# Block sums of the spatial weights: one more set moved up behind the second weight of the first projection

## The chip, the cores and the metric

The kernel runs on one core of one Trainium2 chip. The metric is the device time of one execution in microseconds (us). Engines are named as in the profile: PE is the matrix engine, DVE the vector engine, ACT the scalar engine, POOL the GpSimd engine, SP the engine that here only issues transfers.

## The reference, cut to what matters

```
xn  = layernorm(x)                                   # 2048 x 512
s   = local dilated attention(xn, wqkv) @ wo         # 32 heads, 8 taps at distance 2
z   = gelu(xn @ w_in)                                # 2048 x 1792, halves of 896
z1, z2 = z[:, :896], layernorm(z[:, 896:])
g   = w_sp @ z2 + b_sp                               # w_sp is 2048 x 2048
out = x + s * silu((z1 * g) @ w_out)
```

Everything is float32. The kernel gets that precision by cutting each operand in a high and a low part and by three matmuls for each product.

## The kernel before, in words

The work on PE comes in this order: the projections to q, k and v; the **first projection** (z1, the loop over `f` in seven weights `w1_0` to `w1_6`, lines 693 to 713); the second projection (z2, `z2_half`); the product with `w_sp`, whose 2 x 2 blocks are multiplied in seven products instead of eight (`block_product`), for which sums of weight blocks are needed; the product with `w_out`; the product with `wo`. Attention itself is elementwise work on DVE and POOL, given the lowest priority, and fills DVE wherever nothing else is due there.

**Sets of block sums.** A set `(a, i)` of `block_sums` loads four 128 x 512 blocks of `w_sp` with two transfers of 512 KB each (tiles `sa` and `sb`, line 398, issued by SP), makes four sums on DVE (line 393) and stores the two tiles in `sums_d` (line 403, issued by POOL). `z1_sums` lists eight such sets, `(0, 0)` to `(0, 7)`; set 0 stands ahead of the loop over `f`, the others behind the turns of that loop. They are read back much later, in the products `m6`, `m7`, `m5` and `m3`. Other sets (`a` = 1) are made earlier by POOL (`pool_sums`) and, two of them, during z2 (`raw_sums`).

**The z1 tiles.** A turn `f` makes four products of 12 matmuls each, one for each `c`, every one in a bank of its own of the eight PSUM banks (`mm` goes round them). ACT takes each out with a Gelu (line 707) into half of a tile `z1t_f_0` (c = 0, 1) or `z1t_f_2` (c = 2, 3), and each full tile is stored in `z1_d` (line 709; the profile calls it `z_d`). I number the products n = 4 f + c. Product n + 8 uses the bank of product n, and the first z2 product is n = 28.

**The slots.** The tiles `sa`, `sb`, `z1t` and later `zt` (z2 before its norm) share one pool of eight slots of 512 KB, `t4`. A slot comes free when the last reader is through, which for all but `zt` is the store to memory. The program's order of instructions is set when it is built: each engine's list is filled in the order of the source (attention last), by a planner that works with modelled times, and a free slot goes to the first in that order that can use one. On the chip each engine then works through its list in order, and a tile waits for the slot that the planner gave it. In the kernel before, the program's buffer addresses give this succession ("z20" is `z1t_2_0`, "s2a" the tile `sa` of set 2; behind the arrow the tile that had the slot before):

```
first tenants: s0a s0b z00 z02 s1a s1b z10 z12
s2a<-z00  s2b<-z02  z20<-z10  z22<-s0a  s7a<-s1a  s7b<-z12  s3a<-s0b  s3b<-s1b
z30<-z20  z32<-z22  s4a<-s2a  s4b<-z30  z40<-s2b  z42<-z32  s5a<-s7a  s5b<-s7b
z50<-s3a  z52<-s3b  s6a<-z40  s6b<-z42  z60<-z50  z62<-z52  zt0<-s4a  zt8<-s4b
```

Of the kernel before, what the change touches and what calls it, by code (L numbers as in the profile page):

```python
# [24 lines left out]
FB = FH // P  # L25
# [32 lines left out]
def kernel(  # L58
# [96 lines left out]
    def mm(name):  # L155
        return ps.tile([P, 512], F32, tag=f"bank{next(turn)}", name=name)
# [15 lines left out]
    def side_pair(name):  # L172
        return [wts.tile([P, CT], F32R, tag=f"w{n}", name=name + n) for n in "hl"]

    def prep(src, n, name, raw=None, pair_=None):
        if raw is None:
            raw = fetch(src, n, name)
        hi, lo = pair_ or weight_pair(name)
        split(hi[:, :n], lo[:, :n], raw[:, :n])
        return hi, lo  # L180
# [214 lines left out]
    def block_sums(a, i, tile_=None, eng=nc.vector, loads=nc.sync, stores=nc.scalar, behind=None):  # L395
        top, low = [(tile_ or t4)(f"s{n}_{a}_{i}") for n in "ab"]
        for t, r in ((top, 0), (low, HT)):
            ins = loads.dma_start(t, w_sp[2 * a : 2 * a + 2, r + i].rearrange("c p t -> p c t"))
            if behind:
                tc.add_manual_dep(ins.ins, behind[0].ins.name, behind[1], reason="sums later")  # L400
        added([top[:, 0], top[:, 1], low[:, 0], low[:, 1]], eng)
        for r, t in enumerate((top, low)):
            stores.dma_start(sums_d[a, r, i], t)
# [15 lines left out]
    z1_sums = [(0, i) for i in range(HT)]  # L419
# [104 lines left out]
    def t4(name, n=2):  # L524
        t = wide.tile([P, 2 * CT], F32, tag="t4", name=name, bufs=WIDE)
        return t.rearrange("p (i t) -> p i t", i=2)[:, :n]
# [161 lines left out]
    def first_sums(a, i):  # L688
        block_sums(a, i, stores=nc.gpsimd)
# [3 lines left out]
    for f in range(FB):  # L693
        pair_ = side_pair("w1_last") if f == FB - 1 else None
        wh, wl = prep(w_in1[:, f, :], KB * P, f"w1_{f}", pair_=pair_)
        for c in range(NC):
            pz = mm(f"z1_{f}_{c}")
            for k in range(KB):
                cc = slice(k * P, (k + 1) * P)
                xh, xl = [planes[:, FB - KB + k, c * JC : (c + 1) * JC, a] for a in range(2)]  # L700
                nc.tensor.matmul(pz, wh[:, cc], xh, start=k == 0, stop=False)
                nc.tensor.matmul(pz, wh[:, cc], xl, start=False, stop=False)
                nc.tensor.matmul(pz, wl[:, cc], xh, start=False, stop=k == KB - 1)
            if c % 2 == 0:
                zp = t4(f"z1t_{f}_{c}")
            zt = zp[:, c % 2]
            nc.scalar.activation(zt, pz, AF.Gelu_apprx_tanh)  # L707
            if c % 2:
                nc.scalar.dma_start(z1_d[f, c - 1 : c + 1].rearrange("c p t -> p c t"), zp)
        if f == 2:  # L710
            first_sums(*z1_sums[FB])
        if f < FB - 1:
            first_sums(*z1_sums[f + 1])

    HALF = (slice(0, 512), slice(512, FH))
    WID = (512, FH - 512)
# [119 lines left out]
    for n in range(8):  # L836
        a, f = n // 2 % 2, n // 4 * 2 + n % 2
# [339 lines left out]
```

## Time and profile before

| what | value |
|---|---|
| median of 3 runs | 698.64 us (696.42 to 698.93) |
| the profiled execution: its own time | 696.63 us |
| the profiled execution: span | 694.8 us, so 1.83 us lie around the span |
| mean granted PE clock | 0.999 |
| busy share of the span | PE 99%, DVE 90%, ACT 40%, POOL 31% |
| moved by DMA | 182.36 MB, 262 GB/s on the mean over the span |

A row of the timeline gives the start, the duration, the engine, the line, the operation, output and input, the count, and in square brackets how long the engine had been idle before it and what it had waited for. `SPq` and `ACTq` rows are transfers being issued. A row of the windows gives, for a stretch of the span, its length, then the busy time of each engine with the count of instructions, the granted PE clock, the busy share of the DMA engines and the rate. A row of the waits gives the total in us, how often, and the longest.

### The profile page before, as it was taken

How to read it: one execution, taken by the hardware profiler on the slowest of the kernel's cores; microseconds unless marked ns; L12 is line 12 of the kernel's file. 1: busy time of each engine (PE TensorE's matmuls, PEld its weight loads, DVE VectorE, ACT ScalarE, POOL GpSimd, SP SyncE). 2: the span in 40 equal slices, each digit the busy share in tenths (PEclk: the TensorE clock that was granted, in tenths of full speed). 3: DMA queues.
4: the chain of work that ended last, by engine and by line, in shares of the span. 5: the costliest groups of instructions: out<-in, count | busy, mean ns of one | idle time of the engine just before them, and what ended most of it. 6: DMA issues, size and time to landing. Idle time of an engine off the chain costs nothing.

```text
span 694.8 us, 9233 instructions
## 1 busy us (share of the span) xinstructions
PE 688.0 (99%) x3084; PEld 572.9 (82%) x3084; DVE 624.9 (90%) x866; ACT 276.2 (40%) x458; POOL 213.3 (31%) x242
## 2 busy tenths in 40 slices
PE   8999999999999999999999999999999999999998
PEld 7888888888888899977888888888888887888886
DVE  6777877999999989899999998999998999999875
ACT  4343333314424256765533544342433444211432
POOL 3105737282343321223123222214021111452320
PEclk9999999999999999999999999999999999999999
DMA  8869899959999865266798878667576683645797
GB/s 269 253 191 303 273 361 374 334 200 352 406 410 363 320 227 189 96 212 221 260 401 281 289 222 305 203 224 264 158 255 215 221 306 118 242 155 167 253 339 267
DMA packets 102223, 182.36 MB, mean 262 GB/s; under 512 B 9184, under 2 KB 45280, under 8 KB 102176
## 3 DMA queue, kind: packets, MB, share of 16 engines
q1 hardware_dynamic: 56624, 102.21, 43.7%
q0 software_dynamic: 13824, 52.24, 20.8%
q10 hardware_dynamic: 31728, 27.33, 11.6%
q8 instruction: 24, 0.39, 0.2%
q14 instruction: 23, 0.19, 0.1%
HBM read 122.42 MB, written 59.32 MB: 262 GB/s over the span
## 4 chain that ended last, share of the span: by engine, by line
PE 68%; DVE 15%; DMA 8%; issue 4%; ACT 3%; POOL 1%; DVEq 0%; ACTq 0%; POOLq 0%; SPq 0%
PE g L823 35%; PE qkv L385 4%; PE qkv L387 4%; PE qkv L386 4%; PE b L1066 4%; PE b L1065 4%; PE b L1067 4%; DMA sb<-in_w_sp 3%; DVE lg L580 2%; DVE pr L573 2%; PE s L1066 2%; PE s L1067 2%; PE s L1065 2%; DMA sums_d<-sb 2%; PE qkv L308 2%
## 5 line engine op out<-in xcount | busy, mean ns | idle before, releaser
L631 POOL TENSOR_TENSOR pv<-pv 128x1024 f32<-128x1024 f32 x29 | 69.6, 2400 | 97.1 <-DVE pv L620 85.1
L573 DVE TENSOR_TENSOR pr<-k,q 128x2048 f32<-128x2048 f32 x32 | 73.6, 2300 | 4.3 <-DMA k<-qkv_d 4.1
L620 DVE TENSOR_TENSOR pv<-v,lg 128x2048 f32<-128x2048 f32 x32 | 74.6, 2331 | 0.9 <-DMA v<-qkv_d 0.4
L580 DVE TENSOR_REDUCE lg<-pr 128x128 f32<-128x2048 f32 x32 | 73.0, 2280 | 0.1
L645 POOL DMA_DIRECT2D o_d<-tt x32 | 18.0, 562 | 141.4 <-DVE tt L644 140.9
L433 ACT ACTIVATE stage<-qkv 128x512 f32<-128x512 f32 x40 | 23.0, 590 | 29.7 <-DMA qkv_d<-stage 19.7
L805 POOL DMA_DIRECT2D ol<-o_d x32 | 17.7, 555 | 36.8 <-DVE BIG L197 11.0
L707 ACT ACTIVATE z1t<-z 128x512 f32<-128x512 f32 x28 | 15.5, 596 | 28.9 <-DMA z_d<-z1t 13.5
L728 PE MATMUL z<-w_0h,BIG 128*128 128x512 f32 x64 | 25.0, 391 | 0.8 <-ACT zt L731 0.8
L1076 ACT ACTIVATE bt<-b 128x512 f32<-128x512 f32 x16 | 9.3, 594 | 39.8 <-PE b L1067 39.8
L730 PE MATMUL z<-w_0h,BIG 128*128 128x512 f32 x64 | 25.0, 391 | 0.0
L729 PE MATMUL z<-w_0l,BIG 128*128 128x512 f32 x64 | 25.0, 391 | 0.0
L752 ACT ACTIVATE zt<-zt,nmz,mvz 128x896 f32<-128x896 f32 x16 | 17.5, 1131 | 18.5 <-POOL nmz L746 18.5
L740 DVE BATCH_NORM_STATS2 zst<-zt 128x6 f32<-128x448 f32 x32 | 19.3, 613 | 6.1 <-ACT zt L731 6.0
L280 DVE TENSOR_TENSOR xT<-xT,mr 128x512 f32<-128x512 f32 x20 | 13.8, 688 | 11.8 <-DMA mr<-mv_d 6.8
L636 DVE TENSOR_TENSOR pv<-pv 128x512 f32<-128x512 f32 x32 | 22.9, 716 | 0.0
L731 ACT ACTIVATE zt<-z 128x512 f32<-128x512 f32 (+1 forms) x32 | 15.9, 536 | 14.2 <-DMA sums_d<-sa 12.8
L730 PE MATMUL z<-w_1h,BIG 128*128 128x384 f32 x64 | 21.5, 336 | 0.0
L728 PE MATMUL z<-w_1h,BIG 128*128 128x384 f32 x64 | 21.5, 335 | 0.0
L729 PE MATMUL z<-w_1l,BIG 128*128 128x384 f32 x64 | 21.4, 335 | 0.0
L195 ACT ACTIVATE BIG<-zl 128x512 fp32r<-128x512 f32 x20 | 12.4, 629 | 22.4 <-DVE zl L893 20.6
L393 POOL TENSOR_TENSOR sb<-sa,sb 128x512 f32<-128x512 f32 x12 | 18.7, 1560 | 5.3 <-DMA sb<-in_w_sp 5.0
(478 smaller groups left out, 2303.6 us busy)
## 6 DMA issues: line engine op xcount, KB each, us to landing
qkv_d<-stage ACTq DMA_DIRECT2D x24, 512.0 KB
v<-qkv_d POOLq DMA_DIRECT2D x14, 704.0 KB, 5.3
k<-qkv_d POOLq DMA_DIRECT2D x13, 704.0 KB, 6.4
sums_d<-sa POOLq DMA_DIRECT2D x14, 512.0 KB, 7.5
sums_d<-sb POOLq DMA_DIRECT2D x14, 512.0 KB, 7.8
z_d<-z1t ACTq DMA_DIRECT2D x14, 512.0 KB
zl<-z_d SPq DMA_DIRECT2D x12, 512.0 KB
tr<-t_d SPq DMA_DIRECT2D x12, 384.0 KB
```

What stands on the lines that cost most here:

```text
L385: nc.tensor.matmul(pq, xh[:, k], wh, start=k == 0, stop=False)
L573: line(nc.vector.tensor_tensor(pr, taps(ks[u], j0), qb.unsqueeze(1).to_broadcast([P, W, NJ * CS]), op=ALU.mult))
L580: line(nc.vector.tensor_reduce(lgs[u][:, :, j0 * HS : (j0 + NJ) * HS], pr.rearrange("p w (i d) -> p w i d", d=DH), axis=AX.X, op=ALU.add,))
L620: line(nc.vector.tensor_tensor(pv.rearrange("p w (i d) -> p w i d", d=DH), taps(vs[u], j0).rearrange("p w (i d) -> p w i d", d=DH), lgs[u] ...
L631: eng.tensor_tensor(pv[:, 0:4], pv[:, 0:4], pv[:, 4:8], op=ALU.add)
L728: nc.tensor.matmul(pz, xh[:, k], wh, start=k == 0, stop=False)
L729: nc.tensor.matmul(pz, xh[:, k], wl, start=False, stop=False)
L730: nc.tensor.matmul(pz, xl[:, k], wh, start=False, stop=k == KB - 1)
L823: nc.tensor.matmul(pg, z[a], w[b], start=start and i == 0, stop=stop and i == 2, skip_group_check=seeded)
L1065: nc.tensor.matmul(pp[:, cols], hi, wh, start=k == 0, stop=False)
L1066: nc.tensor.matmul(pp[:, cols], hi, wl, start=False, stop=False)
L1067: nc.tensor.matmul(pp[:, cols], lo, wh, start=False, stop=k == n - 1)
```

## The change: which set stands behind which weight

The order of the eight sets in the source becomes 0 1 2 6 3 7 4 5; before it was 0 1 2 7 3 4 5 6. Behind the turns of the loop stand:

| behind the weight `f` | 0 | 1 | 2 | 3 | 4 | 5 | 6 |
|---|---|---|---|---|---|---|---|
| before | 1 | 2 | 7, 3 | 4 | 5 | 6 | none |
| after | 1 | 2, 6 | 3, 7 | 4 | 5 | none | none |

```diff
-        if f == 2:
-            first_sums(*z1_sums[FB])
-        if f < FB - 1:
+        if f < FB - 2:
             first_sums(*z1_sums[f + 1])
+        if f in (1, 2):
+            first_sums(*z1_sums[f + FB - 2])
```

The work itself is the same: eight sets, the same transfers, the same sums, the same matmuls.

## The prediction, as put on record

> **What bounds the kernel now.** I read the page's head, then busy time by stretches and the waits of PE, then ACT, SP and POOL in order of time through the first projection.
>
> ```profile
> span 694.8 us, 9233 instructions
> PE 688.0 (99%) x3084; PEld 572.9 (82%) x3084; DVE 624.9 (90%) x866; ACT 276.2 (40%) x458; POOL 213.3 (31%) x242
> ...
> 0.00:21.75 21.75, 20.00 (x93) 16.45 (x94) 14.84 (x40) 9.21 (x14) 6.57 (x14) 1.00 0.88 290
> 21.75:230.00 208.25, 208.25 (x928) 172.82 (x927) 178.64 (x213) 69.93 (x121) 90.63 (x90) 1.00 0.91 318
> 230.00:240.00 10.00, 9.22 (x47) 8.05 (x46) 9.86 (x13) 2.19 (x5) 3.49 (x3) 1.00 1.00 399
> 240.00:290.00 50.00, 50.00 (x249) 44.84 (x248) 44.31 (x94) 31.30 (x50) 11.16 (x21) 1.00 0.51 178
> 290.00:330.00 40.00, 39.10 (x176) 32.08 (x175) 37.36 (x60) 26.96 (x45) 11.39 (x12) 1.00 0.58 188
> 330.00:690.00 360.00, 360.00 (x1591) 297.44 (x1589) 338.22 (x446) 136.64 (x226) 90.05 (x102) 1.00 0.73 247
> 690.00:694.80 4.80, 1.38 (x13) 1.23 (x11) 1.70 (x4) 0.00 (x0) 0.00 (x0) 0.82 0.31 109
> ...
> PE z L728 <- ACT zt L731: 0.8, 1, 0.8
> ```
>
> The first number behind the length is PE's busy time. PE has no gap from 21.75 to 230, from 240 to 290 and from 330 to 690. Its idle time is 1.75 us at the head, 0.78 from 230 to 240, 0.90 from 290 to 330 and 3.42 at the tail. Head and tail are out of this change's reach, so the most that it could give back is 0.78 + 0.90 = 1.68 us, or 0.24%, and only the 0.78 lies in the stage that it touches. What it can cost has no such bound: PE runs on only while ACT empties the banks in time, and ACT waits for slots of `t4`.
>
> ```profile
> 175.91 1.09 ACT L707 ACTIVATE z1t<-z 128x512 f32<-128x512 f32 x2 [9.64 <-DMA z_d<-z1t]
> 182.63 0.60 ACT L707 ACTIVATE z1t<-z 128x512 f32<-128x512 f32 x1 [5.63 <-DMA sums_d<-sa]
> ...
> 187.83 1.09 ACT L707 ACTIVATE z1t<-z 128x512 f32<-128x512 f32 x2
> ...
> 204.21 1.09 ACT L707 ACTIVATE z1t<-z 128x512 f32<-128x512 f32 x2 [8.36 <-DMA sums_d<-sb]
> ...
> 216.31 1.09 ACT L707 ACTIVATE z1t<-z 128x512 f32<-128x512 f32 x2
> ...
> 236.70 0.98 ACT L731 ACTIVATE zt<-z 128x512 f32<-128x512 f32 x2 [12.08 <-DMA sums_d<-sa]
> ```
>
> These are n = 8 and 9 (z20), 10 (z22), 12 and 13 (z30), 16 and 17 (z40), 20 and 21 (z50), then zt0. Three of the waits end with a store of block sums; the last of them is what stalls PE for 0.78 us, just before ACT starts on zt0 at 236.70. When a bank is due is read from the first matmul of a weight, the number ahead of "to":
>
> ```profile
> L701 PE MATMUL z<-BIG,w_2h x16: 389/389/389, 162.7 to 172.9; 128*128 128x512 f32 x16
> L701 PE MATMUL z<-BIG,w_4h x16: 389/389/389, 184.5 to 194.7; 128*128 128x512 f32 x16
> L701 PE MATMUL z<-BIG,w_5h x16: 389/389/389, 195.4 to 205.6; 128*128 128x512 f32 x16
> L701 PE MATMUL z<-BIG,w_lasth x16: 389/389/389, 206.2 to 216.4; 128*128 128x512 f32 x16
> ...
> L728 PE MATMUL z<-w_0h,BIG x64: 387/389/502, 217.1 to 290.6; 128*128 128x512 f32 x64
> ```
>
> From weight 2 (n = 8, 162.7) to the first z2 product (n = 28, 217.1) are 20 products in 54.4 us, 2.72 us each. Bank n is due when product n + 8 starts, and it is empty one ACT step (0.60) after the wait ends. So the reserve is 184.5 - 176.5 = 8.0 us at n = 8, 195.4 - 188.4 = 7.0 at n = 12, 206.2 - 204.8 = 1.4 at n = 16 and 217.1 - 216.9 = 0.2 at n = 20. PE doesn't stall there, but at n = 16 and 20 it nearly does. The z1 stage is not short of matmul time; it is short of slots.
>
> **The change part by part.** Work: nothing is added or removed. A set is two issues on SP, four sums on DVE and two issues on POOL:
>
> ```profile
> 185.24 0.37 SPq L398 DMA_DIRECT2D sa<-in_w_sp  x1
> 185.71 0.44 SPq L398 DMA_DIRECT2D sb<-in_w_sp  x1
> ...
> 198.74 0.42 SPq L398 DMA_DIRECT2D sa<-in_w_sp  x1
> ...
> 221.77 0.38 SPq L398 DMA_DIRECT2D sa<-in_w_sp  x1
> ...
> 193.56 0.99 DVE L393 TENSOR_TENSOR sb<-sa,sb 128x512 f32<-128x512 f32 x1
> ...
> 175.56 1.14 POOL L403 DMA_DIRECT2D sums_d<-sa  x2 [0.79 <-DVE sa L393]
> ...
> 189.71 0.54 POOL L403 DMA_DIRECT2D sums_d<-sa  x1
> ...
> 194.96 0.53 POOL L403 DMA_DIRECT2D sums_d<-sb  x1 [0.44 <-DVE sb L393]
> ...
> DMA to landing us min/median/max: 2.9/9.1/11.7
> ...
> 170.00:230.00 60.00, 17.16 (x26) 0.00 (x0) 1.00 1.02 393
> 230.00:250.00 20.00, 6.77 (x10) 0.00 (x0) 1.00 0.72 285
> ```
>
> The last two rows are windows of line 393 alone (DVE, then POOL): 17.16 us / 26 = 0.66 us a sum, so 2.6 us of DVE a set, and 0.8 of SP and 1.1 of POOL by the rows above. This work moves up about 40 us (set 6 was loaded last, at 221.77) and costs nothing by itself: on DVE it displaces attention, which has the rest of the kernel to catch up (DVE idles 360 - 338.2 = 21.8 us from 330 to 690). If that cover were gone, the price would be 2.6 us. Behind SP's two issues stand raw weight loads for z2 and later. Behind POOL's stores, which wait for DVE's sums, stand attention's loads and folds. Both hit attention first, not PE. Bounds for them: 0, and 2.6 + 1.1 = 3.7 us if all of a set's DVE and POOL time came through; I take 0, nearest to the rows, as DVE has the 21.8 in hand.
>
> Slots: this is the term that counts. Two tiles more stand ahead of z20 and of every z1 tile up to z52 (a second set behind `f` = 1; from `f` = 2 on, the count of sets stays one ahead until `f` = 5). z60 and zt0 have as many ahead as before. If slots come free in the same succession, set 6 takes those of z10 and s0a, and z20 gets s1a's, z22 z12's, z30 s2a's, z32 s2b's.
>
> - z20: in the kernel before, s1a's slot went to set 7, whose load was issued at 185.24, 9.7 us after the stores of sets 0 and 1 (175.56). So bank 8 is empty at 185.24 + 0.60 = 185.84 and was due at 184.5: PE stalls 1.3 us.
> - z30 behind s2a: stored at 189.71, and the slot's next load went out at 198.74. Empty by 199.3, due at 195.4: late by 3.9 us at most.
> - z32 behind s2b: stored at 194.96, its end released ACT at 204.21. Empty at 204.8; n = 14 is due with n = 22, 195.4 + 2 x 2.72 = 200.8: late by 4.0 us.
> - z50, reserve 0.2 us: two tiles more ahead. From z20 to zt0 (positions 11 to 31 of the succession) slots were passed on from 175.91 to 236.70, 3.0 us each, so two are 6.1 us, less 0.2: 5.9 us late.
>
> These don't add up: a stall shifts PE for good and gives all later banks as much more time, so the largest counts. On the other side the planner may put set 6's sums early, and DVE took set 2's last sum (193.56) long after its load; z30 and z32 need then not wait for it. Below nothing the term can't go, as PE had no stall here before. Its bounds are thus 0 and 5.9 us. I take 1.3, the first of these rows: it rests on one step of inference, the others on the planner's repeating everything up to there.
>
> The stall at zt0: the eight sets are now all placed ahead of z50, zt0's slots don't wait for the store of a set in its last third, and any stall before gives it that much more time. I count it as gone, -0.78 us (bounds -0.78 and 0). Late next at that place is bank 29 by the same ACT chain, at 237 to 238, which has the same cover. The 0.90 us from 290 to 330 I leave: the same z2 work precedes it.
>
> Sum: +1.3 - 0.8 = +0.5 us on the profiled execution, 696.63 to about 697.1 (span 694.8 to 695.3). That execution was 2.0 us under the median of the runs; on the median, 698.64 + 0.5 = 699.1 us.
>
> The step rests on how long a store holds its slot: 2.9 to 11.7 us, median 9.1, in the row above. [...]
>
> **The rivals.**
>
> *The stall only goes (a gain).* Place: zt0 at 236.70. The planner finds slots for z20 to z52 in time, for instance by giving z20 the slot of z12, or since set 6, landing earlier, is also summed earlier. Then -0.8 us, and up to -1.7 if DVE, with two sets fewer in z2, also frees the 0.90 at 290 to 330: 697.9 to 697.0 us. For it: from 230 to 250 DMA falls to 0.72 busy and DVE still makes 10 sums there. Against: reserves of 1.4 and 0.2 us. It decides if z40 and z50 come no later than now.
>
> *DMA is the bound of the stage (a loss).* Place: z1, weights 3 to 5. A set is 1 MB in and 1 MB out, 2.1 MB at 393 GB/s is 5.3 us; with DMA full from 170 to 230, whatever stands behind the moved set lands 5.3 us later, z50 among it, where 0.2 us are in reserve. PE stalls 5.3 - 0.2 = 5.1, less 0.78: +4.3 us, 702.9; by the slot count above +5.1, 703.7; if only z32's wait for s2b comes true, +3.2, 701.8. It decides from 4.3 us of stall on (then +3.5 is passed). [...]
>
> *It doesn't do what it says.* SP's list is in order and set 6 waits there for slots. If those come free no sooner than for set 7 now (185.24, against 175.91 for z10's), sets 6 and 7 only swap names: 0, 698.6 us. Against: z10's slot, free at 175.91, is ahead in the succession.
>
> **How the numbers follow.** About 0.5%, 3.5 us, is what a measurement of this kernel can tell from no change. Forecast, stalls move ahead and cost from 0.8 less to 3 more than they gave: 0.36, with a range of its own of 697.9 to 701.6. The gain: 0.26. DMA or slots as the bound: 0.28. Nothing: 0.10. Faster by over 3.5 us would take twice the idle time that PE has within reach: 0.03. Slower by over 3.5: nearly all of the DMA case and little else, 0.28. Within: 0.69. The range of 8 in 10 takes in -1.7 from the gain and +5.1 from the loss, 696.9 to 703.7.
>
> **What would show it.** Right: the idle of PE at zt0 near 237 is gone; a new one of 1 to 2 us stands between 184 and 200, with ACT's z1t (line 707) waiting for a store of sums; SP issues set 6's loads, the fourth pair, by 186; from 21.75 on PE idles 0.5 us more in all. The gain shows as no PE gap between 140 and 290. The DMA case shows as PE idle of 4 us or more at weights 3 to 6, with a DMA share near 1.0 up to 225 and lower after. The prediction is wrong in kind if the planner reorders attention so that PE waits from 290 on or at the tail, since attention's last transpose stands 29 us before the end of the span, or if a store of a set still ends zt0's wait.
>
> ```profile
> 665.81 0.44 DVE L644 STREAM_TRANSPOSE tt<-pv 128x256 f32<-128x256 f32 x1
> ```

## The result, and the profile after

| | before | changed |
|---|---|---|
| median, runs side by side | 697.58 us (696.03 to 698.93, 7 runs) | 700.84 us (699.79 to 702.57, 7 runs) |
| ratio | 1 | 1.006, 95% interval 1.0045 to 1.0075 |
| profiled execution: its own time | 696.63 us | 702.32 us |
| its span and mean granted PE clock | 694.8 us, 0.999 | 700.2 us, 0.994 |

The change makes the kernel 0.6% slower, 3.3 us on the median. A second comparison gave 699.90 against 695.61 us, ratio 1.0058 (1.0040 to 1.0076). The profiled execution is at the slow end of the changed kernel's runs: 5.7 us above the profiled execution of before, where the medians stand 3.3 us apart. Its mechanisms can be read from it; their full size belongs to that execution.

The windows of the changed kernel (PE, PEld, DVE, ACT, POOL busy; PE clock, DMA share, GB/s) and its waits from 140 to 690:

```profile
185.00:200.00 15.00, 11.34 (x49) 8.93 (x48) 15.00 (x18) 4.91 (x8) 5.67 (x7) 1.00 1.02 374
200.00:230.00 30.00, 28.67 (x114) 23.49 (x115) 29.83 (x43) 12.98 (x22) 11.88 (x15) 0.89 1.00 378
230.00:240.00 10.00, 10.00 (x52) 8.94 (x51) 9.99 (x12) 2.73 (x7) 3.51 (x3) 1.00 1.03 408
290.00:330.00 40.00, 40.00 (x188) 34.42 (x187) 36.79 (x56) 28.18 (x46) 11.42 (x13) 1.00 0.60 196
...
PE z L701 <- ACT z1t L707: 5.0, 2, 4.1
```

PE's gaps at 230 to 240 and at 290 to 330 are gone (10.00 and 40.00 busy, where 9.22 and 39.10 stood). New idle time of 5.0 us stands between 185 and 202, in two stalls, both on ACT's `z1t`. And from 200 to 230 PE has a granted clock of 0.89 where it had 1.00. In order of time, ACT, then POOL, then PE:

```profile
185.43 1.09 ACT L707 ACTIVATE z1t<-z 128x512 f32<-128x512 f32 x2 [10.80 <-DMA sums_d<-sa]
...
188.06 1.28 ACT L606 ACT_TABLE_LOAD   x1
...
199.39 1.28 ACT L707 ACT_TABLE_LOAD   x1 [9.19 <-issue]
200.68 1.09 ACT L707 ACTIVATE z1t<-z 128x512 f32<-128x512 f32 x2
```

```profile
190.41 0.54 POOL L403 DMA_DIRECT2D sums_d<-sa  x1
```

```profile
186.07 0.50 PE L701 MATMUL z<-BIG,w_4h 128*128 128x512 f32 x1 [0.91 <-ACT z1t L707]
...
201.33 0.80 PE L701 MATMUL z<-BIG,w_5h 128*128 128x512 f32 x1 [4.08 <-ACT z1t L707]
201.93 0.63 PE L702 MATMUL z<-BIG,w_5h 128*128 128x512 f32 x1
202.35 0.63 PE L703 MATMUL z<-BIG,w_5l 128*128 128x512 f32 x1
...
207.04 0.51 PE L702 MATMUL z<-BIG,w_5h 128*128 128x512 f32 x1
207.39 0.39 PE L703 MATMUL z<-BIG,w_5l 128*128 128x512 f32 x1
207.62 0.40 PE L701 MATMUL z<-BIG,w_5h 128*128 128x512 f32 x1
```

The first ACT row is z20 (n = 8), behind the store of s1a. The 4.08 us are z30 (n = 12): its slot is s2a's, POOL issued that store at 190.41, and ACT came on only at 199.39. Even then 1.28 us of table load stood ahead of the Gelu, because softmax's exponential (line 606) had changed the tables at 188.06. The row calls the 9.19 us "issue"; that they are the wait for s2a's store follows from the program's buffer addresses, in which z30 has the slot of s2a, and the 9.0 us between 190.41 and 199.39 are what such stores took before (median 9.1).

Behind that stall the matmuls start 0.43 us apart (201.93, 202.35) until 207.04, and 0.23 apart from 207.39 on. From 201.93 to 207.04 the granted clock is 0.50. Fourteen matmuls at 0.20 us too much are 2.8 us. Behind the 0.91 us stall nothing slows down (granted clock 1.00 from 186.07 to 190.00).

Where the time went is read from the starts of the stages:

```profile
L701 PE MATMUL z<-BIG,w_4h x16: 389/389/497, 186.1 to 196.4; 128*128 128x512 f32 x16
L701 PE MATMUL z<-BIG,w_5h x16: 389/389/796, 201.3 to 214.4; 128*128 128x512 f32 x16
L701 PE MATMUL z<-BIG,w_lasth x16: 389/389/389, 215.1 to 225.3; 128*128 128x512 f32 x16
L728 PE MATMUL z<-w_0h,BIG x64: 387/389/390, 226.0 to 298.4; 128*128 128x512 f32 x64
L823 PE MATMUL g<-ws_0h,BIG x52: 389/389/389, 391.3 to 563.1; 128*128 128x512 f32 x52
L1065 PE MATMUL s<-BIG x16: 389/389/389, 652.4 to 662.6; 128*128 128x512 f32 x16
```

The last two of the kernel before:

```profile
L823 PE MATMUL g<-ws_0h,BIG x52: 389/389/389, 385.2 to 557.0; 128*128 128x512 f32 x52
L1065 PE MATMUL s<-BIG x16: 389/389/389, 647.0 to 657.2; 128*128 128x512 f32 x16
```

Against before, weight 4 starts 1.6 us later (186.1 against 184.5), weight 5 5.9, the last weight 8.9, z2 8.9, the end of z2 7.8 (298.4 against 290.6), the first `ws_0h` 6.1, the product with `wo` 5.4, and the span is 5.4 longer. So 8.9 are lost by the start of z2: 5.0 of stalls, 2.8 of clock, and 1.1 with no stall beside them, 0.7 of it ahead of weight 4. Of this, 0.5 stands already at the first weight (141.5 against 141.0), ahead of anything that was moved, and so belongs to the execution and not to the change. And 3.5 us come back: 1.1 in z2, 1.7 up to `ws_0h`, 0.7 up to `wo`. Idle time of before that is gone makes 1.68 of them (0.78 at 237 and 0.90 from 290 to 330).

### The profile page after: what moved, and what is told of

The parts are those of the page before. It is cut to its first block, busy times and chain, and to the rows that moved or that the text cites. A ratio compares the mean times of both kernels' runs of the same rounds, so it can differ in the third digit from the quotient of the medians.

```text
span 700.2 us, 9238 instructions
## 1 busy us (share of the span) xinstructions
PE 689.1 (98%) x3084; PEld 575.0 (82%) x3084; DVE 624.9 (89%) x866; ACT 279.4 (40%) x458; POOL 213.4 (30%) x242
## 4 chain that ended last, share of the span: by engine, by line
PE 72%; DVE 12%; DMA 9%; issue 4%; ACT 1%; SPq 1%; POOL 1%; DVEq 0%; ACTq 0%; POOLq 0%
PE g L823 39%; PE z L730 4%; PE z L729 4%; PE z L728 4%; PE b L1067 4%; PE b L1065 4%; PE b L1066 4%; DMA qkv_d<-stage 3%; PE s L1067 2%; PE s L1066 2%; PE s L1065 2%; DMA sb<-in_w_sp 2%; DVE pv L620 1%; DMA xT<-in_x_t 1%; PE qkv L308 1%
## 5 line engine op out<-in xcount | busy, mean ns | idle before, releaser
L744 POOL TENSOR_TENSOR mvz<-mvz,nhalf 128x2 f32<-128x2 f32 x8 | 8.2, 1019 | 45.6 <-DVE mvz L743 45.6
L197 DVE TENSOR_TENSOR BIG<-zt,BIG 128x512 fp32r<-128x512 f32 (+2 forms) x24 | 18.4, 778 | 3.7 <-ACT BIG L195 3.7
L823 PE MATMUL g<-ws_0h,BIG 128*128 128x512 f32 x52 | 20.2, 389 | 0.0
```

The costliest lines, as they stand in the source:

```text
L823: nc.tensor.matmul(pg, z[a], w[b], start=start and i == 0, stop=stop and i == 2, skip_group_check=seeded)
```

## The experiments

Three theories. **Slots:** z1 tiles wait for stores of sums, and what counts is the succession in the pool. **Full DMA:** the moved transfers themselves are what PE waits for. **DVE's order:** the planner writes DVE's list anew for each edit, and what is won or lost ahead of z2 changes hands at 290 to 330, where PE waits for DVE's low parts of the `w_sp` blocks. Ratios are to the kernel before, run side by side on the same chip, with 95% intervals.

**One half of the change: one more set behind the second weight.** The third then has one, and the sixth keeps its set; order 0 1 2 7 3 4 5 6.

```diff
-        if f == 2:
-            first_sums(*z1_sums[FB])
-        if f < FB - 1:
-            first_sums(*z1_sums[f + 1])
+        for i in {0: (1,), 1: (2, 7), 2: (3,), 3: (4,), 4: (5,), 5: (6,)}.get(f, ()):
+            first_sums(*z1_sums[i])
```

> One half of the change alone: set 7 moves up behind the second weight (order 0 1 2 7 3 4 5 6, with 2 and 7 behind f = 1), the last set stays behind the sixth. Theory A (slots: a z1 tile that has to wait for the store of a block sum holds a bank, PE stalls, and a stall of 4 us also halves PE's clock for some 6 us): the program's buffer addresses give z20 the slot of s1a, as in the changed kernel, but z30 that of z20 and z32 that of z22, not those of set 2. So a stall of about 0.9 us near 185, none of 4 us near 197, no stretch at half the clock; the 0.8 us at zt0 may stay. Time: 0 to 1 us over the kernel before, 697.6 to 698.6. Theory B (DMA is full from 170 to 230, and 2.1 MB moved ahead of the z1 tiles delay them all): the same load moves ahead as in the changed kernel, so a stall of 4 us or more and about 3 us over the kernel before, 700.8.

Measured: 696.52 us, ratio 1.0016 (1.0000 to 1.0032), profiled span 694.8, as before.

```profile
185.00:200.00 15.00, 15.00 (x68) 12.38 (x67) 15.00 (x19) 8.38 (x14) 5.66 (x7) 1.00 1.04 403
200.00:230.00 30.00, 30.00 (x138) 25.25 (x137) 29.62 (x40) 9.53 (x16) 11.29 (x14) 1.00 1.01 374
```

DMA is as full as in the changed kernel (1.04 and 1.01), and PE has no gap in these stretches. A set is loaded earlier, but only ahead of the tiles of the third weight (z20 and z22); from z30 on as many sets stand ahead as before, where the changed kernel keeps one more. In this program z20 has s1a's slot as in the changed kernel, but z30 has z20's and z32 has z22's. So a full DMA with one more set ahead of z20 does not stall PE there, and s1a's slot for z20 need not cost anything: the 1.3 us that the prediction took is not the term. The 0.9 us stall that was expected near 185 did not come.

**The other half: none behind the sixth.**

```diff
 ...
+        for i in {0: (1,), 1: (2,), 2: (7, 3), 3: (4,), 4: (5, 6)}.get(f, ()):
+            first_sums(*z1_sums[i])
```

> The other half alone: set 6 moves up one place, behind the fifth weight (7 and 3 behind f = 2, 4 behind f = 3, 5 and 6 behind f = 4, none behind f = 5). Theory A: z20 to z52 keep the predecessors that they have in the kernel before or get a z1 tile's slot, and zt0 still waits for s4a: no new stall in z1, the 0.8 us at zt0 stays. Time within 0.5 us of the kernel before, 697.1 to 698.1. Theory B: 2.1 MB more ahead of z50, whose bank had 0.2 us in reserve: a stall of up to 5 us near 217, 700 to 702.

Measured: 697.54 us, ratio 1.0027 (1.0008 to 1.0046).

```profile
PE g L821 <- DVE wsp_1l L197: 1.9, 1, 1.9
PE z L726 <- ACT zt L729: 1.0, 1, 1.0
```

The first projection has no new stall, and zt0's stall remains. In the profile the largest wait stands at the seam between z2 and `w_sp`, 1.9 us; that execution took 700.37 us, the longest of the twelve, so the size is its own. Neither half has the changed kernel's stalls: those come with both, two sets behind the second weight and still two behind the third. By the addresses of the changed program, set 7 then takes z20's and z22's slots, and z30 and z32 are left with set 2's.

**The z1 tiles out of the pool.** The changed kernel with all z1 tiles in idle planes of the big operand buffer, in 12 places. That buffer's type is fp32r, so z1 is written as fp32r too.

```diff
 ...
-                zp = t4(f"z1t_{f}_{c}")
+                i = 2 * next(idle)
+                zp = BIG[:, i * CT : (i + 2) * CT].rearrange("p (i t) -> p i t", i=2)
 ...
```

> The changed kernel with its z1t tiles in twelve places of their own, in the three planes of BIG that lie idle during z1; the sets keep the eight slots of t4. All transfers and sums are the same, their order in the source too. z1 is written in the rounded format of those planes, so its low bits are lost; nothing else is left out. Theory A: no z1 tile waits for a set, so PE has no gap between 140 and 290, at zt0 neither, and the clock stays at 1.0: 0.8 to 1.7 us under the kernel before, 696 to 697, and 4 to 5 under the changed one. Theory B: the same bytes stand ahead, so the gaps stay and the time is that of the changed kernel, 700.8.

Measured: 701.85 us, ratio 1.0094 (1.0063 to 1.0125).

```profile
165.00:185.00 20.00, 20.00 (x90) 16.54 (x89) 13.65 (x21) 6.56 (x11) 5.99 (x10) 1.00 1.04 405
```

```profile
PE g L825 <- ACT wsp_1h L195: 2.8, 1, 2.8
PE b L1067 <- ACT wout_4h L195: 1.9, 1, 1.9
PE g L825 <- DVE ws_2l L197: 1.3, 1, 1.3
```

Without slots to wait for, no z1 tile stalls PE, at a DMA share of 1.04. That speaks for slots and against full DMA as the cause. But it is no gain, where 696 to 697 us were expected: the freed slots let four sets be loaded at once (eight issues on SP from 158.05 to 161.61), DVE waits for loads of sets (7.3 us in two waits, 13.65 busy of 20), and PE's waits stand from 290 on. That the late sums cause those waits is not shown, and the profiled execution is the slowest of the six (706.77 us).

**The stall filled.** The changed kernel with 18 more matmuls of 512 columns ahead of product n = 19, whose results are overwritten.

```diff
+            for _ in range({(4, 3): 18}.get((f, c), 0)):
+                nc.tensor.matmul(
+                    pz, wh[:, :P], planes[:, FB - KB, c * JC : (c + 1) * JC, 0], start=True, stop=True
+                )
```

> The changed kernel with 18 matmuls of 512 columns more (18 x 0.227 = 4.1 us) at the head of the product n = 19, overwritten by that product itself, so that PE works in the place where it stood idle for 4.1 us. Theory A with the clock as its second half: PE is no less late, but the clock stays at 1.0 behind it, which in the changed kernel cost 14 matmuls at 0.427 us instead of 0.227, 2.8 us: about 698 to 698.8, 2 to 3 us under the changed kernel. Rival (the slow matmuls behind the stall come from something else, such as the loads and stores then under way): the slow stretch stays and the time is that of the changed kernel, 700.8, or longer by what the fill doesn't fit.

Measured: 701.86 us, ratio 1.0090 (1.0062 to 1.0118); the profiled execution took 699.62.

```profile
PE z L732 <- ACT z1t L711: 1.4, 1, 1.4
PE z L705 <- ACT z1t L711: 0.7, 1, 0.7
```

Two short stalls are left and the granted clock is 1.00 from 165 to 240, so the half clock belongs to the long stall. But nothing is won: z2 starts at 223.2, hardly before the second profile of the changed kernel below (223.5), and the median did not fall to the expected 698 to 698.8. The 1.4 us, just ahead of 223.2, are the first z2 product waiting for ACT on the bank of z50. Its slot is s7a's; that ACT waited for that store is inferred from the addresses. So, by that, where the first stall is filled and the clock stays up, the next tile behind a set holds PE. How much of the changed kernel's median is clock can't be read from this, also because the planner wrote another list for DVE here (see the last experiments).

**Only two tiles out of the pool.** The changed kernel with z30 and z32 in the idle planes (fp32r there, as above).

```diff
 ...
+                if f in (3,):
+                    i = 2 * next(idle)
+                    zp = BIG[:, i * CT : (i + 2) * CT].rearrange("p (i t) -> p i t", i=2)
+                else:
+                    zp = t4(f"z1t_{f}_{c}")
 ...
```

> The changed kernel with only the two tiles z30 and z32 (f = 3) in places of their own, in planes of BIG that are idle during z1; all else keeps its slots (z1 of that weight is written in the rounded format of those planes). Theory A (the stall of 4.1 us and the half clock behind it come from z30's and z32's taking the slots of set 2, whose stores end near 199 and 204): no stall near 197 and no stretch at half the clock; z20's stall of 0.9 near 185 stays, and some new wait at 217 to 230 is possible, since z50 still follows set 7. About 0 to 1.5 us over the kernel before, 2 to 4 us under the changed kernel. Theory B (DMA full, whatever holds the slots): as the changed kernel, some 4 us over the kernel before.

Measured: 700.20 us, ratio 1.0064 (1.0041 to 1.0088).

```profile
209.95 1.09 ACT L712 ACTIVATE z1t<-z 128x512 f32<-128x512 f32 x2 [3.20 <-DMA sums_d<-sa]
```

```profile
210.60 0.79 PE L702 MATMUL z<-BIG,w_lasth 128*128 128x512 f32 x1 [4.18 <-ACT z1t L712]
211.19 0.63 PE L703 MATMUL z<-BIG,w_lasth 128*128 128x512 f32 x1
```

The stall has its old size and a new place: z40, which now stands behind s6a, the very set that the change moves up. Taking two tiles out of the row only passed the wait to the next tile behind a set. The half clock follows it (matmuls of 0.63 us from 211.19 on, for 5.7 us; granted clock 0.89 from 200 to 230). The time expected from the theory of slots, 0 to 1.5 us over the kernel before, was wrong by that passed-on wait; the 4.6 us measured are the number that full DMA would have given too, but z30's stall went with its slot and z40's came with s6a's.

**One wait forced into the kernel before.** z30 waits there for the store of s2a, as in the changed kernel.

```diff
 ...
+            if (f, c) == (3, 0):
+                tc.add_manual_dep(out_of.ins, stored[0, 2, 0].ins.name, SYNC, reason="as if in its slot")
```

> The kernel before, its order of sets untouched, but ACT's step on z30 also has to wait for the store of s2a, as if it had its slot. Theory A: PE stalls at n = 20 for 3 to 4 us, its clock falls to half behind that for some 6 us (2 to 3 us more), while zt0's 0.8 us and the 0.9 us between 290 and 330 go, since PE comes later to both: 3 to 5 us over the kernel before, as the changed kernel. Theory B: no load is moved, so nothing of it: within 1 us of the kernel before.

Measured: 697.38 us, ratio 1.0018 (1.0003 to 1.0034), profiled span 695.6.

```profile
197.86 0.50 PE L703 MATMUL z<-BIG,w_5h 128*128 128x512 f32 x1 [1.93 <-ACT z1t L709]
...
198.90 0.41 PE L704 MATMUL z<-BIG,w_5h 128*128 128x512 f32 x1
199.13 0.60 PE L705 MATMUL z<-BIG,w_5l 128*128 128x512 f32 x1
...
202.77 0.39 PE L705 MATMUL z<-BIG,w_5l 128*128 128x512 f32 x1
```

```profile
L732 PE MATMUL z<-w_0h,BIG x64: 387/389/390, 221.4 to 293.8; 128*128 128x512 f32 x64
```

The wait alone makes the stall, at the predicted place, and again a slow stretch behind it, which begins 1.3 us after PE is running again (197.86 to 199.13; granted clock 0.96 from 200 to 230). z2 starts 4.3 us late (221.4 against 217.1), yet the span grows by 0.8: 3.5 us come back here too. So the median is only 1.8 us above, where 3 to 5 were expected. The planner gave later tiles other slots in this program, so it isn't the wait alone from there on.

**The changed kernel again**, on the chip of the last two and the next.

> The changed kernel once more, beside the others on one chip. Both theories: about 0.6% over the kernel before. [...]

Measured: 699.90 us, ratio 1.0058 (1.0040 to 1.0076), profiled execution 699.66.

```profile
183.60 1.09 ACT L707 ACTIVATE z1t<-z 128x512 f32<-128x512 f32 x2 [9.61 <-DMA sums_d<-sa]
...
196.38 1.28 ACT L707 ACT_TABLE_LOAD   x1 [8.01 <-issue]
```

```profile
188.65 0.54 POOL L403 DMA_DIRECT2D sums_d<-sa  x1
```

```profile
198.33 0.63 PE L701 MATMUL z<-BIG,w_5h 128*128 128x512 f32 x1 [2.89 <-ACT z1t L707]
...
201.75 0.49 PE L703 MATMUL z<-BIG,w_5l 128*128 128x512 f32 x1
...
212.45 0.50 PE L701 MATMUL z<-BIG,w_lasth 128*128 128x512 f32 x1 [1.36 <-ACT z1t L707]
```

```profile
210.07 0.42 ACT L606 ACTIVATE lg<-lg 128x256 f32<-128x256 f32 x1 [6.17 <-DVE lg L601]
210.50 1.28 ACT L707 ACT_TABLE_LOAD   x1
```

z30 stalls PE again, 2.89 us with the same table load ahead of it (the store took 7.7 us this time, 188.65 to 196.38), and the slow stretch ends after 3.4 us (198.33 to 201.75). z20 does not stall (183.60). So z30 is the stall that both profiles have. This one has a second, of 1.36 us at the last weight, and it is not one of slots: ahead of z40 ACT's list has softmax's exponential, which waits for DVE until 210.07, and then a table load. No slow matmuls follow it (starts 0.24 us apart or less from 212.78 on). z2 starts at 223.5, 6.4 us later than in the kernel before, and the span (697.7) is 2.9 longer: 3.5 us come back again. Of the 16 runs of the changed kernel, the two with a granted clock of 0.994 took 701.37 and 702.32 us, the other 14 (0.997 to 0.999) 698.62 to 702.57. The kernel before has 0.998 to 1.000. A difference of 0.001 to 0.002 of some 700 us is an estimated 0.7 to 1.4 us of the 3.3 that go to the clock in a usual run, and about 3 us in the profiled one.

**Only zt0's stall taken away.** The kernel before with z60 and z62 in the idle planes (fp32r there, as above), so that zt0 and zt8 get z1 slots.

```diff
 ...
+                if f in (6,):
+                    i = 2 * next(idle)
+                    zp = BIG[:, i * CT : (i + 2) * CT].rearrange("p (i t) -> p i t", i=2)
 ...
```

> The kernel before with the tiles z60 and z62 (f = 6) in idle planes of BIG, so that zt0 and zt8 take the slots of z50 and z52 and wait for no set (z1 of that weight is written in the rounded format). By the sum in the prediction, the 0.8 us at zt0 go and nothing comes back: 0.8 us under the kernel before. Theory C (from 290 to 330 DVE is what PE waits for, so whatever PE wins in z1 or z2 it loses there): PE's idle time at 237 goes to 0 and that from 290 to 330 rises from 0.9 to about 1.7: the time of the kernel before.

Measured: 702.02 us, ratio 1.0092 (1.0065 to 1.0119).

```profile
PE g L828 <- DVE wsp_1l L197: 2.3, 1, 2.3
PE g L828 <- ACT g L846: 1.5, 1, 1.5
```

zt0's stall is gone, and the kernel is 0.9% slower. A removed 0.8 us stall bought nothing: PE waits 2.3 us at the seam, 1.5 between 310 and 330 and another 2.4 from 330 on, more than any theory expected.

**PE made late by work, with the old order.** The 3.5 us that come back in the changed kernel might come back whenever PE is late. So the kernel before gets the same filling, of 4.1 and of 8.2 us, and passes its slots on as before up to z60.

```diff
+            for _ in range({(4, 3): 18}.get((f, c), 0)):      # 36 in the second
+                nc.tensor.matmul(
+                    pz, wh[:, :P], planes[:, FB - KB, c * JC : (c + 1) * JC, 0], start=True, stop=True
+                )
```

> The kernel before with 18 more matmuls of 512 columns (4.1 us by the pitch of 0.2267 us) at the head of product n = 19, whose results are overwritten: PE reaches the second projection 4.1 us later without any wait, and the slots of the pool pass on in the old succession up to zt0. The question is whether a delay of PE in the first projection is partly given back later, whatever causes it. Given back (DVE is late behind PE by 290 to 330, so that a later PE finds its data ready there): z2 starts about 4 us later (221.2), no idle at zt0 and at 290 to 330, the span only about 0.6 us longer (4.1 less 3.5), ratio 1.000 to 1.002. Not given back (what the changed kernel regained came from its other order of the sums): z2 starts 4.1 later, at most the 0.8 at zt0 goes, the span about 3.3 us longer, ratio 1.005.

> The same with 36 more matmuls, 8.2 us. Given back up to a fixed amount of about 3.5 us: the span 4.7 us longer, ratio 1.006 to 1.007. Not given back but for the 0.8 at zt0: 7.4 us longer, ratio 1.0105. If still more than 3.5 us were given back, DVE's lateness behind PE would be larger than the runs so far showed, and the ratio would be below 1.005.

Measured: 704.20 us, ratio 1.0131 (1.0100 to 1.0162), and 706.27 us, ratio 1.0162 (1.0138 to 1.0185). Both lie above every number expected. In the first, z2 starts 4.5 us late, PE waits for `wsp_1l` at the seam, and the span is 702.1, 7.3 more than before:

```profile
L732 PE MATMUL z<-w_0h,BIG x64: 387/389/390, 221.6 to 294.0; 128*128 128x512 f32 x64
```

```profile
PE g L827 <- DVE wsp_1l L197: 2.4, 1, 2.4
```

When DVE makes that operand, in this kernel, in the changed one and in the one before, in that order:

```profile
301.89 0.69 DVE L197 TENSOR_TENSOR wsp_1l<-wsp_1r,wsp_1h 128x512 fp32r<-128x512 f32 x1
```

```profile
298.10 0.64 DVE L197 TENSOR_TENSOR wsp_1l<-wsp_1r,wsp_1h 128x512 fp32r<-128x512 f32 x1
```

```profile
296.15 0.64 DVE L197 TENSOR_TENSOR wsp_1l<-wsp_1r,wsp_1h 128x512 fp32r<-128x512 f32 x1
```

In the changed kernel PE is 7.8 us late at the end of z2 and DVE's operand only 2.0 us, so PE finds it ready. In the filled one PE is 4.5 us late at the start of z2 and the operand 5.7, so nothing comes back.

That does not settle whether lateness of PE gives something back, because the filled programs differ in more than the filling. From the place of `wsp_1l` on, DVE's list has 500 instructions. In the built programs 226 and 230 of these places hold another instruction in the two filled kernels than in the kernel before; in the changed kernel only one neighbouring pair has changed places, and with the forced wait none has. With the forced wait, z2 starts as late as in the first filled kernel (221.4 against 221.6), but DVE makes the operand at 295.40, PE does not wait, and 3.5 us come back:

```profile
295.40 0.65 DVE L197 TENSOR_TENSOR wsp_1l<-wsp_1r,wsp_1h 128x512 fp32r<-128x512 f32 x1
```

Over all the experiments the ratios go with this list: the five programs that keep the old one from `wsp_1l` on, to within that pair (the changed one, its two halves, two tiles out of the pool, the forced wait), have ratios up to 1.0064, and the five that have another one (z1 tiles out of the pool, the stall filled, zt0's stall taken away, the two filled here) 1.0090 and more. So 3.5 us were seen to come back where PE was late and DVE kept its old list at the seam, and no run separates the two causes. The old list is not a condition: the changed kernel with the filled stall has another one, and in its profiled execution 3.4 us come back too (z2 at 223.2, 6.1 late; span 2.7 longer). Why the planner writes the other list, and where the part of the 3.5 us beyond the 1.68 of idle time comes from, stays open.

## Why the prediction was right, and where it was off

The measured 700.84 us lies in the range of the forecast's own case (697.9 to 701.6) and 1.7 above its number. The direction was stated as a loss of 0.5 us within the noise; it is a loss of 3.3 that the runs can tell. That it still lies in the range is in part luck: 8.9 and 6.4 us were lost by the start of z2 in the two profiles, more than the forecast's own case allowed, and 3.5 us that the prediction did not have came back. By its steps:

- **The bound.** That the first projection is short of slots and not of DMA held: z1 tiles without slots run without a stall at a DMA share of 1.04 (third experiment), one more set ahead of z20 and z22 does too (first), and the forced wait makes the stall with no set moved. The rival of full DMA saw its sign come true, PE idle of 4 us or more in these weights (5.0 and 4.3) at a share near 1.0, but for another reason; its times, 701.8 to 703.7, lie above the median.
- **The succession of slots.** Set 6 takes the slots of z10 and s0a, z20 stands behind s1a, z22 behind z12, z30 behind s2a, z32 behind s2b: the changed program's addresses have exactly this.
- **z20, predicted 1.3 us, taken as the term.** 0.91 in one profile, none in the other, none in the first experiment. The size was fair, the choice was not.
- **z30, predicted "late by 3.9 us at most", kept as a bound.** This is the step that failed: it measured 4.08 and 2.89 us. The prediction chose z20 because it "rests on one step of inference". But the succession was one inference for all rows, and by the prediction's own rule, "the largest counts", the term was not the smallest of four rows, and z30 was larger than z20. The 4.08 come about differently from the 3.9: PE was already 1.85 late (due at 201.33 - 4.08 = 197.25 and not at 195.4), and the bank was empty at 201.3 and not at 199.3, since the slot came some 0.7 later and a table load of 1.28 stood behind the wait. In the kernel before, PE waited for nothing there.
- **"These don't add up."** True of z32 and z50: both still waited for a store, and PE had no stall there. Not quite true of z20 and z30: both stalled, since the first moves ACT's list back as well as PE's due time. The rule itself held: z50, the largest row ("5.9 us late"), had its bank empty at 225.1 and 223.1 in the two profiles, 8.0 and 6.0 us after the 217.1 at which it was due before, and PE came 0.9 and 0.4 us later still. Where the stall was filled, z50 is what PE waited for (1.4 us). So z30's stall and the half clock came mostly in place of a stall at z50, and the largest row was the nearest to what was lost by z2.
- **The half clock, not priced at all.** 2.8 us in the profiled execution, an estimated 0.7 to 1.4 in a usual one. z50's bank was empty only 0.9 us before PE came, so the profiled execution would have won an estimated 0.9 at most without the half clock. The traces show the half (0.43 against 0.23 us from start to start; granted clock 0.50 from 201.93 to 207.04) behind stalls of 1.93, 2.89, 4.08 and 4.18 us, for 3.4 us behind the first two and 5.7 behind the others. How long a stall it takes, and what sets its length, no run shows.
- **zt0's stall, -0.78.** It is gone; z2 gained 1.1.
- **The 0.90 at 290 to 330, left in place.** Wrong in sign: with the rest of the stretch 1.7 us came back there. The reason given, that the same z2 work precedes it, left out that PE arrives later (7.8 us at the end of z2) and finds DVE's operand, 2.0 us later, ready.
- **The moved work on DVE, POOL and SP, 0.** Nothing in the trace asks for more, but no run measures it by itself.
- **How long a store holds its slot: 2.9 to 11.7 us, median 9.1.** It held: s2a's took 9.0 us (190.41 to 199.39) and, in the second profile, 7.7 (188.65 to 196.38), from POOL's issue to ACT's next step.

In sum, for the profiled execution: predicted 1.3 - 0.8 = +0.5; measured 5.0 of stalls + 2.8 of clock + 1.1 other - 3.5 back = +5.4. The places were right, the larger rows were left as bounds, the clock was forgotten, and the give-back behind z2 was not seen.

## What to carry to other kernels

Where a pool hands its slots on in a list, write out who follows whom before and after a change, and price every tile whose predecessor changes from a quickly freed buffer to one that waits for a slow store (7.7 and 9.0 us here); take the largest of them, not the surest, and add what the waiting engine has to do behind its wait (here a table load of 1.28 us). Look for slow time behind a stall of the matrix engine: in the first projection here 3.4 us at the half clock stood behind stalls of 1.93 and 2.89 us and 5.7 behind those of 4.08 and 4.18, none behind 0.91 and 1.36. And where a planner writes the lists anew, a stall that is removed is not yet time that is won: here a kernel without zt0's stall, and one without any stall in the first projection, were both slower than the kernel before. Both had another list on DVE: compare the lists of two programs before a run is read as a test of one cause.

## What the runs showed of the hardware that was not expected

- Stalls of 1.93, 2.89, 4.08 and 4.18 us in the first projection were each followed by matmuls at half rate (0.43 us from start to start where the others have 0.23), for about 3.4 us behind the first two and 5.7 behind the other two; those of 0.91 and 1.36 us were not. At the seam behind z2, the kernel with no set behind the sixth weight has a granted clock of 0.50 (300 to 302) after a wait of 1.90 us, and the one without zt0's stall keeps 1.00 (290 to 310) with a wait of 2.3 us. Behind the 1.93 us stall the slow stretch began only 1.3 us after PE was running again (197.86 to 199.13).
- The same store of 512 KB in the same program took 9.0 us in one execution and 7.7 in another, and z30's stall behind it 4.08 and 2.89 us.
